# The operands of the final stage: loaded behind the last group of the stage before, in its buffers

## The chip, the core and the metric

The kernel runs on one core of a Trainium2 chip, in one launch. The metric is the device time of that launch in microseconds (us), lower is better. The time before is 6255.53 us, the median of three runs (6249.93 to 6257.06). The profile is of a separate run of 6245.49 us, whose span from first to last instruction is 6243.7 us.

## What is computed

The reference is the forward pass and the gradients of a gated mixture of two attention blocks over one sequence of 2048 tokens with width 576. Block A is attention of 32 heads with 18 channels each, which share one key and one value head. Block B is a recurrence over 64 segments of 32 tokens with 8 memory rows, 32 heads of 128 channels. In short:

```python
g = sigmoid((x * gate_w).sum(-1, keepdims=True))        # x is A_x
a = softmax_attention(x @ wq, x @ wk, x @ wv) @ wo      # block A
b = memory_recurrence(B_x, mem0, Wq, Wk, Wv, Wo)        # block B
out = g * a + (1 - g) * b
grads = vjp(out)(grad_out)   # of A_x, wq, wk, wv, wo, mem0, Wq, Wk, Wv, Wo, gate_w
```

The end of the kernel, which is what matters here, computes the weight gradients of block B, the output and the gate's gradient, and then, for block A:

```
dx     = dq @ wq.T + dkv @ wkv.T + dz * gate_w + dxB    (output 1)
d wq   = x.T @ dq                                       (output 2)
d wk, d wv = x.T @ dkv.T                                (outputs 3 and 4)
d wo   = o.T @ da                                       (output 5)
```

Here dq, dkv, o and da come from the backward pass of block A and lie in DRAM since long before; dz is the gradient of the gate's argument, one number for each token, and dxB is what block B adds.

## The kernel before

The program is a series of stages, each with its own pools of SBUF and PSUM tiles: projections, the forward recurrence woven with attention A, bulk work of B, the backward recurrence woven with the backward pass of A, `b_post`, then the two stages of interest, `b_dw` and `a_final`. A pool is given back at the end of its `with` block, and a later pool may lie on the same memory; its first instructions then wait for whatever still uses that memory.

`b_dw` runs 16 groups, k = 0 to 15: four weight gradients (Wo, Wq, Wk, Wv) by four pairs of column blocks of 512. The contraction is over 20 row tiles, 16 of tokens and 4 of memory rows. Operand one is `w_d`, 128 x 20 x 512 in bf16, with four buffers: two in use and two being loaded, since `load(k + 1)` is issued at the start of group k. Operand two is `w_h`, 128 x 20 x 576 in bf16, with two buffers: one holds db and the memory's gradient for k below 4, the other holds x (`A_x`, its first 16 row tiles) and the memory rows for all groups after. Each group makes nine products (20 matmuls each in the first eight) into the PSUM tile `w_acc` (six buffers of one bank), `evac` copies each out on VectorE (DVE) and ScalarE (ACT) in turn to `w_o16` (four buffers), and GpSimd (POOL) issues the store. After each group `gate(k)` computes row tile k of the output and of dz, from tiles that `gate_load` requested at the group's start: `o_b` and `o_go` through GpSimd, `o_T` through SyncE (SP).

After group 15 the gradient of gate_w is made: `dz_all` is cast to `w_dz`, 32 matmuls multiply it with the x part of `w_h`, two DVE copies make `w_dg` (L1199) and SyncE stores it (L1200).

`a_final` then loads all that it needs (L1623 to L1640): gate_w broadcast over partitions, five token tensors of 128 x 16 x 576 (x, dq, ot, da, dxb, 2304 KB each, on SyncE and GpSimd in turn), wq, wkv and dkv. wkv is made by 20 small loads on GpSimd, with a memset ahead. It transposes wq and wkv on TensorE (PE) (`f_wtr`, one PSUM buffer), brings dkv into token order (`f_pk`), and goes over 16 row tiles for dx: transposes of dq (`f_ptr`, two buffers), products into `f_big` (two buffers of two banks), `f_dx32` on DVE, `f_dx16` on GpSimd, the store on SyncE for even tiles and GpSimd for odd ones. Then, for five row tiles of the weights, it makes the products x.T @ dq, o.T @ da and x.T @ dkv.T.

Within `b_dw` the order of instructions on each engine is that of the program (`manual_schedule`). `a_final` has no such block: there a scheduler orders the instructions when the kernel is built. [...] Matmuls and transposes all pass through two helpers and so carry L66 and L71; copies by `evac` carry L61 (DVE) and L63 (ACT). Their tile names tell them apart.

Of the kernel before, what the change touches and what calls it, by code (L numbers as in the profile page):

```python
# [9 lines left out]
BF16 = mybir.dt.bfloat16  # L10
F32 = mybir.dt.float32
P = 128

D = 576
NKT = 5
# [15 lines left out]
class Kern:  # L31
# [1067 lines left out]
    def b_dw(self, sp, psum):  # L1099
        nc = self.nc  # L1100
        NTT = self.NTT
        n = NTT + self.NM // P
        WS = ("o", "dq", "dk", "dv")

        def load(k):
            which, jp = WS[k // 4], k % 4
            ts = []
            for jc in (2 * jp, 2 * jp + 1):
                cs = slice(jc * 512, (jc + 1) * 512)
                t = sp.tile([P, n, 512], BF16, name="w_d", bufs=4)  # L1110
                nc.sync.dma_start(t[:, 0:NTT, :], self.xtok[which][:, cs].rearrange("(n p) d -> p n d", p=P))
                if k < 4:
                    for mt in range(self.NM // P):
                        nc.sync.dma_start_transpose(
                            t[:, NTT + mt, :].rearrange("p (h e) -> p h e", e=E),
                            self.oh_dram[mt][:, 4 * jc:4 * jc + 4, :].rearrange("e h t -> e (h t)"))
                else:
                    nc.sync.dma_start(t[:, NTT:n, :], self.mtok[which][:, cs].rearrange("(n p) d -> p n d", p=P))
                ts.append((t, cs))
            return ts  # L1120

        def load_h(xs, ms):
            ht = sp.tile([P, n, D], BF16, name="w_h", bufs=2)
            nc.sync.dma_start(ht[:, 0:NTT, :], xs.rearrange("(n p) d -> p n d", p=P))
            nc.sync.dma_start(ht[:, NTT:n, :], ms.rearrange("(n p) d -> p n d", p=P))
            return ht

        def groups(k, ts, ht):
            if k < 4:
                od = self.outs[10].rearrange("h e d -> (h e) d")  # L1130
                for t, cs in ts:
                    for i in range(4):
                        acc = [psum.tile([P, 512], F32, name="w_acc", bufs=6) for _ in range(2)]
                        for it in range(n):
                            for hf in range(2):
                                self.mm(acc[hf][:, 0:288], lhsT=t[:, it, 128 * i:128 * i + 128],
                                        rhs=ht[:, it, 288 * hf:288 * hf + 288], start=(it == 0), stop=(it == n - 1))
                        o16 = sp.tile([P, D], BF16, name="w_o16b", bufs=3)
                        for hf in range(2):
                            self.evac(o16[:, 288 * hf:288 * hf + 288], acc[hf][:, 0:288])  # L1140
                        r0 = cs.start + i * 128
                        nc.gpsimd.dma_start(od[r0:r0 + 128, :], o16[:, :])
                        yield
                return
            od = self.outs[6 + k // 4].rearrange("d h e -> d (h e)")
            for t, cs in ts:
                for kt in range(4):
                    acc = psum.tile([P, 512], F32, name="w_acc", bufs=6)
                    for it in range(n):
                        self.mm(acc[:], lhsT=ht[:, it, kt * P:kt * P + P], rhs=t[:, it, :],  # L1150
                                start=(it == 0), stop=(it == n - 1))
                    o16 = sp.tile([P, 512], BF16, name="w_o16", bufs=4)
                    self.evac(o16[:], acc[:])
                    nc.gpsimd.dma_start(od[kt * P:kt * P + P, cs], o16[:])
                    yield
            acc = psum.tile([P, 512], F32, name="w_acc", bufs=6)
            for it in range(n):
                for i, (t, cs) in enumerate(ts):
                    self.mm(acc[64 * i:64 * i + 64, :], lhsT=ht[:, it, 512:576], rhs=t[:, it, :],
                            start=(it == 0), stop=(it == n - 1), tp=(0, 64 * i))  # L1160
            o16 = sp.tile([P, 512], BF16, name="w_o16", bufs=4)
            self.evac(o16[:], acc[:])
            for i, (t, cs) in enumerate(ts):
                nc.gpsimd.dma_start(od[512:576, cs], o16[64 * i:64 * i + 64, :])
            yield

        with self.tc.manual_schedule():
            ht = load_h(self.db_dram, self.dm_dram)
            nxt = load(0)
            wo = sp.tile([P, NKT, D], BF16, name="w_wo", bufs=1)  # L1170
            nc.vector.memset(wo[64:128, 4, :], 0.0)
            nc.gpsimd.dma_start(wo[:, 0:4, :], self.A_wo[0:512, :].rearrange("(k p) d -> p k d", p=P))
            nc.gpsimd.dma_start(wo[0:64, 4, :], self.A_wo[512:D, :])
            mem = None
            for k in range(16):
                ts = nxt
                if k % 4 == 0 and k < 12:
                    mem = self.mem_tok(k // 4, sp, psum, 2)
                    next(mem)
                if k < 15:  # L1180
                    nxt = load(k + 1)
                if k == 1:
                    hx = load_h(self.A_x, self.mem_dram)
                gl = self.gate_load(k, sp)
                for _ in groups(k, ts, ht):
                    next(mem, None)
                self.gate(k, gl, wo, sp, psum)
                if k == 3:
                    ht = hx
            dz16 = sp.tile([P, NTT], BF16, name="w_dz", bufs=1)  # L1190
            nc.vector.tensor_copy(dz16[:], self.dz_all[:])
            pg = [psum.tile([P, 512], F32, name="w_acc", bufs=6) for _ in range(2)]
            for tt in range(NTT):
                for hf in range(2):
                    self.mm(pg[hf][0:1, 0:288], lhsT=dz16[:, tt:tt + 1], rhs=ht[:, tt, 288 * hf:288 * hf + 288],
                            start=(tt == 0), stop=(tt == NTT - 1))
            dg16 = sp.tile([P, 2, 288], BF16, name="w_dg", bufs=1)
            for hf in range(2):
                nc.vector.tensor_copy(dg16[0:1, hf, :], pg[hf][0:1, 0:288])  # L1199
            nc.sync.dma_start(self.outs[11][None, :], dg16[0:1].rearrange("p a b -> p (a b)"))  # L1200

    def setup_A_dram(self, dram):
        T = self.T
# [412 lines left out]
            for i, (l, r) in enumerate(pairs):  # L1616
                self.mm(out[:, lo:hi], lhsT=l, rhs=r[:, lo:hi], start=(i == 0), stop=(i == n - 1))

    def a_final(self, keep, sp, psum):
        nc = self.nc  # L1620
        T, NTT = self.T, self.NTT
        gwb = keep.tile([P, D], BF16, name="f_gwb")
        nc.sync.dma_start(gwb[:], self.gate_w.partition_broadcast(P))  # L1623
        tok = {}
        for i, (nm, src) in enumerate((("x", self.A_x), ("dq", self.dqtok_dram), ("ot", self.otok_dram),
                                       ("da", self.da_dram), ("dxb", self.dxB_dram))):
            t = keep.tile([P, NTT, D], BF16, name="f_" + nm)
            (nc.sync if i % 2 == 0 else nc.gpsimd).dma_start(t[:], src[:, 0:D].rearrange("(n p) d -> p n d", p=P))
            tok[nm] = t
        wq = keep.tile([P, NKT, D], BF16, name="f_wq")  # L1630
        wkv = keep.tile([P, NKT, P], BF16, name="f_wkv")
        nc.gpsimd.memset(wkv[:], 0.0)
        for kt in range(NKT):
            rows = KT_ROWS[kt]
            r = slice(kt * P, kt * P + rows)
            nc.sync.dma_start(wq[0:rows, kt, :], self.A_wq[r, :])
            for i in range(4):
                nc.gpsimd.dma_start(wkv[0:rows, kt, 32 * i:32 * i + DA], (self.A_wk if i < 2 else self.A_wv)[r, :])
        dkv = keep.tile([P, T], BF16, name="f_dkv")
        nc.sync.dma_start(dkv[:], self.dkv_dram[:, :])  # L1640
        wqT = keep.tile([P, NKT, D], BF16, name="f_wqT")
        wkvT = keep.tile([P, D], BF16, name="f_wkvT")
        for kd in range(NKT):
            drows = KT_ROWS[kd]
            ptr = psum.tile([P, 640], BF16, name="f_wtr", bufs=1)
# [6 lines left out]
            rows = KT_ROWS[kt]  # L1652
            self.tr(ptr[:, kt * P:kt * P + rows], wkv[0:rows, kt, :], rows)
        self.evac(wkvT[:, :], ptr[:, 0:D])
        dkt = keep.tile([P, NTT, 36], BF16, name="f_dkt")
        for t4 in range(NTT // 4):
            pk = psum.tile([P, 4, 36], F32, name="f_pk", bufs=1)
            for j in range(4):
# [34 lines left out]
def build_full(tc, A_x, A_wq, A_wk, A_wv, A_wo, B_mem0, B_Wq, B_Wk, B_Wv, B_Wo, gate_w, grad_out, outs_raw,  # L1693
               dbg=None):
    nc = tc.nc
    T = A_x.shape[1]
# [3 lines left out]
    k = Kern(tc, T, A_x, A_wq, A_wk, A_wv, A_wo, B_mem0, B_Wq, B_Wk, B_Wv, B_Wo, gate_w, grad_out, outs=outs)  # L1700
    PS = lambda name, bufs=1: tc.tile_pool(name=name, bufs=bufs, space=bass.MemoryType.PSUM)
    SB = lambda name, bufs=1: tc.tile_pool(name=name, bufs=bufs)
    with SB("const") as cpool, tc.tile_pool(name="dram", bufs=1, space=bass.MemoryType.DRAM) as dram:
# [38 lines left out]
        with SB("tw") as tw:  # L1742
# [4 lines left out]
                    k.weave(k.b_chain_bwd(rk, rs, rp), k.a_pass2(a3k, a3s, a3p), 1)  # L1747
            with SB("yk") as yk, SB("ys") as ys, PS("yp") as yp:
                k.b_post(yk, ys, yp)
        with SB("ws") as ws, PS("wp") as wp_:  # L1750
            k.b_dw(ws, wp_)
        with SB("a5k") as a5k, SB("a5s") as a5s, PS("a5p") as a5p:
            k.a_final(a5k, a5s, a5p)
    return k


# [74 lines left out]
```

The softmax here doesn't subtract the row's maximum and nothing guards it: scores larger than these inputs give would overflow.

## Time and profile before

| What | Value |
|---|---|
| Time, median of three | 6255.53 us |
| Span of the profiled run | 6243.7 us |
| PE busy over the span | 5691.9 us (91%) |
| DVE, ACT, POOL busy | 60%, 56%, 31% |
| Last group of `b_dw` and its gate on PE, end | about 6104 us |
| Matmuls for the gradient of gate_w | 6106.8 to 6110.9 us |
| Last of the two `w_dg` copies ends | 6111.6 us |
| First transpose of wq (`f_wtr`) | 6153.5 us |
| Last matmul of the kernel ends | 6239.2 us |

Times inside the profile count from the first instruction of the span. In a chain of waits each row gives a start, a duration and the work that held up the end in that time; SPq is the SyncE queue issuing a DMA. In a timeline, the bracket after a row is the idle time before it and what ended that. In the windows, each engine's busy us stand with the number of its instructions in brackets, then the granted TensorE clock (1.00 is full), the share of time in which the 16 DMA engines were busy, and GB/s.

### The profile page before, as it was taken

How to read it: one execution, taken by the hardware profiler on the slowest of the kernel's cores; microseconds unless marked ns; L12 is line 12 of the kernel's file. 1: busy time of each engine (PE TensorE's matmuls, PEld its weight loads, DVE VectorE, ACT ScalarE, POOL GpSimd, SP SyncE). 2: the span in 40 equal slices, each digit the busy share in tenths (PEclk: the TensorE clock that was granted, in tenths of full speed). 3: DMA queues.
4: the chain of work that ended last, by engine and by line, in shares of the span. 5: the costliest groups of instructions: out<-in, count | busy, mean ns of one | idle time of the engine just before them, and what ended most of it. 6: DMA issues, size and time to landing. Idle time of an engine off the chain costs nothing.

```text
span 6243.7 us, 208736 instructions
## 1 busy us (share of the span) xinstructions
PE 5691.9 (91%) x88611; PEld 3321.0 (53%) x88822; DVE 3743.0 (60%) x7061; ACT 3500.1 (56%) x5105; POOL 1952.9 (31%) x3451
## 2 busy tenths in 40 slices
PE   7898999999999985999869999999998999899996
PEld 5443444444444434777735555555554777674443
DVE  4336777777777773666558888888887111121111
ACT  3326787778777873656557777777776222111101
POOL 3002343434343342444423333333333111122213
PEclk9999999999999997999989999999999999999998
DMA  4646666666675536999864444444444999996643
GB/s 153 223 151 120 126 125 127 126 127 125 127 125 107 105 85 181 249 257 258 245 207 107 109 109 108 108 111 109 110 108 103 244 244 250 243 261 196 222 150 114
DMA packets 1368111, 991.97 MB, mean 159 GB/s; under 512 B 931613, under 2 KB 1184806, under 8 KB 1356486
## 3 DMA queue, kind: packets, MB, share of 16 engines
q1 hardware_dynamic: 1285030, 780.53, 52.1%
q0 software_dynamic: 82144, 198.05, 10.0%
q8 instruction: 696, 11.40, 0.8%
q14 instruction: 241, 1.97, 0.1%
HBM read 552.41 MB, written 384.76 MB: 150 GB/s over the span
## 4 chain that ended last, share of the span: by engine, by line
PE 64%; ACT 15%; issue 9%; DMA 6%; SPq 3%; POOL 2%; DVE 1%; ACTq 0%; POOLq 0%; DVEq 0%
ACT b_E L1564 10%; PE w_acc L66 10%; PE a_acc L66 8%; PE c_x L66 6%; PE b_S L66 6%; PE a_S L66 5%; PE c_pj L66 5%; PE p_pb L66 4%; PE r_pj L66 4%; ACT a_E L1422 3%; PE r_x L66 2%; DMA dsx_dram<-x_dS 2%; PE x_tr L71 2%; PE b_acc L66 2%; PE x_po L66 1%
## 5 line engine op out<-in xcount | busy, mean ns | idle before, releaser
L1455 DVE TENSOR_TENSOR a_W<-a_dP,a_E 128x512 bf16<-128x512 f32 x2048 | 1316.2, 685 | 413.2 <-PE a_dP L66 289.7
L1585 DVE TENSOR_TENSOR b_dS<-b_dP,b_E 128x512 bf16<-128x512 f32 x2048 | 1312.9, 683 | 241.8 <-issue 119.6
L1564 ACT ACTIVATE b_E<-b_S 128x1024 bf16<-128x1024 f32 x1024 | 1048.9, 1024 | 446.3 <-PE b_dP L66 322.0
L1422 ACT ACTIVATE a_E<-a_S 128x1024 bf16<-128x1024 f32 x1024 | 1050.6, 1026 | 218.5 <-PE a_dP L66 182.9
L66 PE MATMUL b_S<-b_KV,b_QD 32*128 32x512 bf16 x2048 | 401.1, 382 | 155.2 <-ACT b_E L1564 100.7
L66 PE MATMUL r_pj<-WT,r_dT 128*32 128x288 bf16 x12288 | 493.5, 287 | 1.5 <-issue 1.5
L66 PE MATMUL w_acc<-w_d,w_h 128*128 128x512 bf16 (+1 forms) x2352 | 471.0, 379 | 2.5
L66 PE MATMUL a_acc<-a_E,l_VK 128*32 128x512 bf16 x4096 | 401.6, 380 | 27.9 <-ACT a_acs L1460 27.8
L66 PE MATMUL a_S<-a_QD,l_KV 32*128 32x512 bf16 x2048 | 398.5, 384 | 24.7 <-ACT a_E L1422 15.3
L66 PE MATMUL b_acc<-b_dS,b_SD 128*32 128x512 bf16 x2048 | 419.3, 391 | 0.6 <-DVE b_dS L1585 0.2
L66 PE MATMUL a_acc<-a_W,l_WK 128*32 128x512 bf16 x4096 | 411.8, 390 | 0.2 <-DVE a_W L1455 0.2
L66 PE MATMUL b_acc<-b_E,b_SD 128*32 128x512 bf16 x2048 | 404.0, 391 | 0.0
L66 PE MATMUL b_dP<-b_KV,b_QD 32*128 32x512 bf16 x2048 | 401.2, 386 | 0.0
L66 PE MATMUL a_dP<-a_QD,l_KV 32*128 32x512 bf16 x2048 | 398.1, 385 | 0.0
L66 PEld LDWEIGHTS <-r_dT 128*32 128x32 bf16 x12288 | 333.2, 97 | 80.5 <-issue 2.6
L1055 DVE COPY y_T<-y_pt 128x512 bf16<-128x512 bf16 x256 | 97.1, 420 | 461.5 <-PE y_pt L71 461.4
L66 PEld LDWEIGHTS <-b_QD 32*128 32x128 bf16 x4096 | 164.9, 91 | 345.7 <-issue 284.7
L66 PEld LDWEIGHTS <-w_h 128*128 128x128 bf16 (+1 forms) x2400 | 213.0, 100 | 244.6 <-issue 3.4
L66 PEld LDWEIGHTS <-hm 128*32 128x32 bf16 x7680 | 188.2, 96 | 186.4 <-issue 14.6
L1041 ACT CAST y_tdk<-y_pk 128x512 bf16<-128x512 f32 x128 | 75.1, 587 | 377.0 <-PE y_pk L66 212.5
L66 PEld LDWEIGHTS <-l_KV 32*128 32x128 bf16 x4096 | 118.9, 91 | 297.4 <-issue 275.3
L66 PE MATMUL y_pdx<-WT,y_T 128*128 128x288 bf16 x2048 | 272.8, 287 | 0.0
(416 smaller groups left out, 11401.9 us busy)
## 6 DMA issues: line engine op xcount, KB each, us to landing
b_QD<-qd_dram SPq DMA_DIRECT2D x256, 128.0 KB
b_SD<-sd_dram SPq DMA_DIRECT2D x256, 128.0 KB
dOx_dram<-p_tok SPq DMA_DIRECT2D x16, 1024.0 KB
c_vx<-vx_dram SPq DMA_DIRECT2D x256, 64.0 KB
krow_dram<-c_k POOLq DMA_DIRECT2D x64, 256.0 KB, 3.0
qrow_dram<-c_q POOLq DMA_DIRECT2D x64, 256.0 KB, 3.4
vrow_dram<-c_v POOLq DMA_DIRECT2D x64, 256.0 KB, 3.0
x_q<-qx_dram SPq DMA_DIRECT2D x32, 512.0 KB
```

The lines of the kernel that those rows point to most:

```text
L66: return self.nc.tensor.matmul(out, lhsT, rhs, start=start, stop=stop, tile_position=tp, skip_group_check=True)
L71: return self.nc.tensor.transpose(out, in_, self.identB[b:b + nrows, b:b + nrows], tile_position=tp)
L1041: nc.scalar.copy(d[w][:, r, :], pk[:])
L1055: nc.vector.tensor_copy(T_[t][w][:], pt[:])
L1422: nc.scalar.activation(E_[n][:], S.pop(n)[:], ACT.Exp, scale=SCALEA)
L1455: nc.vector.tensor_tensor(out=W_[n][:, i, :], in0=dP[i][:], in1=E_[n][:, i, :], op=ALU.mult)
L1564: nc.scalar.activation(E_[n][:], S.pop(n)[:], ACT.Exp, scale=SCALEA)
L1585: nc.vector.tensor_tensor(out=D_[n][:, i, :], in0=dP[i][:], in1=E_[n][:, i, :], op=ALU.mult)
```

## The change

The change lets the final stage take its operands from the buffers of the weight-gradient stage, which stay alive for it, so that loads can be issued before that stage is over.

- x is not loaded a second time: `tok["x"]` is the `w_h` tile that the stage still holds.
- At the start of group 15, after `gate_load`, `final_load` takes the other `w_h` buffer, in which db lay, and packs wq, gate_w, dkv and wkv into it. It also requests dq and dxb into the next two `w_d` buffers.
- After the gradient of gate_w, `final_tok` requests ot and da, which take the last two `w_d` buffers.
- All of these but the small loads of wkv are issued by SyncE; before, dq and da were issued by GpSimd.
- The SBUF pool of `b_dw` stays open around `a_final`; only its PSUM pool is closed. The pool `a5k` is gone; the transposed weights and `f_dkt` lie in `a5s`.

```diff
                 gl = self.gate_load(k, sp)
+                if k == 15:
+                    self.final_load(sp)
                 for _ in groups(k, ts, ht):
...
             nc.sync.dma_start(self.outs[11][None, :], dg16[0:1].rearrange("p a b -> p (a b)"))
+            self.ftok["x"] = ht
+            self.final_tok(sp, ("ot", "da"))
...
-    def a_final(self, keep, sp, psum):
-        gwb = keep.tile([P, D], BF16, name="f_gwb")
-        nc.sync.dma_start(gwb[:], self.gate_w.partition_broadcast(P))
-        tok = {}
-        for i, (nm, src) in enumerate((("x", self.A_x), ("dq", self.dqtok_dram), ("ot", self.otok_dram),
-                                       ("da", self.da_dram), ("dxb", self.dxB_dram))):
-            t = keep.tile([P, NTT, D], BF16, name="f_" + nm)
-            (nc.sync if i % 2 == 0 else nc.gpsimd).dma_start(t[:], src[:, 0:D].rearrange("(n p) d -> p n d", p=P))
-            tok[nm] = t
+    def final_tok(self, ws, names):
+        src = {"dq": self.dqtok_dram, "ot": self.otok_dram, "da": self.da_dram, "dxb": self.dxB_dram}
+        for nm in names:
+            t = ws.tile([P, self.NTT + self.NM // P, 512], BF16, name="w_d", bufs=4)
+            v = t[:].rearrange("p a b -> p (a b)")[:, 0:self.NTT * D].rearrange("p (n d) -> p n d", d=D)
+            self.nc.sync.dma_start(v, src[nm][:, 0:D].rearrange("(n p) d -> p n d", p=P))
+            self.ftok[nm] = v
+    def final_load(self, ws):
+        f = ws.tile([P, self.NTT + self.NM // P, D], BF16, name="w_h", bufs=2)
+        flat = lambda r, n: f[:, r:, :].rearrange("p a b -> p (a b)")[:, 0:n]
+        wq, gwb = f[:, 0:NKT, :], f[:, NKT, :]
+        dkv = flat(6, self.T)
+        wkv = flat(10, NKT * P).rearrange("p (k c) -> p k c", c=P)
+        nc.gpsimd.memset(wkv, 0.0)
         for kt in range(NKT):
...
             nc.sync.dma_start(wq[0:rows, kt, :], self.A_wq[r, :])
             for i in range(4):
                 nc.gpsimd.dma_start(wkv[0:rows, kt, 32 * i:32 * i + DA], (self.A_wk if i < 2 else self.A_wv)[r, :])
+        nc.sync.dma_start(dkv, self.dkv_dram[:, :])
+        nc.sync.dma_start(gwb, self.gate_w.partition_broadcast(P))
+        self.final_tok(ws, ("dq", "dxb"))
...
-        with SB("ws") as ws, PS("wp") as wp_:
-            k.b_dw(ws, wp_)
-        with SB("a5k") as a5k, SB("a5s") as a5s, PS("a5p") as a5p:
-            k.a_final(a5k, a5s, a5p)
+        with SB("ws") as ws:
+            with PS("wp") as wp_:
+                k.b_dw(ws, wp_)
+            with SB("a5s") as a5s, PS("a5p") as a5p:
+                k.a_final(a5s, a5p)
```

More of the change, by code (lines that the diff above doesn't have):

```diff
@@ L1617, in row_mm @@
                 self.mm(out[:, lo:hi], lhsT=l, rhs=r[:, lo:hi], start=(i == 0), stop=(i == n - 1))
-    def a_final(self, keep, sp, psum):
-        nc = self.nc
-        T, NTT = self.T, self.NTT
-        gwb = keep.tile([P, D], BF16, name="f_gwb")
-        nc.sync.dma_start(gwb[:], self.gate_w.partition_broadcast(P))
-        tok = {}
-        for i, (nm, src) in enumerate((("x", self.A_x), ("dq", self.dqtok_dram), ("ot", self.otok_dram),
-                                       ("da", self.da_dram), ("dxb", self.dxB_dram))):
-            t = keep.tile([P, NTT, D], BF16, name="f_" + nm)
-            (nc.sync if i % 2 == 0 else nc.gpsimd).dma_start(t[:], src[:, 0:D].rearrange("(n p) d -> p n d", p=P))
-            tok[nm] = t
-        wq = keep.tile([P, NKT, D], BF16, name="f_wq")
-        wkv = keep.tile([P, NKT, P], BF16, name="f_wkv")
-        nc.gpsimd.memset(wkv[:], 0.0)
+    ftok = {}
+    def final_tok(self, ws, names):
[6 more added lines that the diff above has]
+    def final_load(self, ws):
+        nc = self.nc
+        f = ws.tile([P, self.NTT + self.NM // P, D], BF16, name="w_h", bufs=2)
[4 more added lines that the diff above has]
+        nc.gpsimd.memset(wkv, 0.0)
         for kt in range(NKT):
@@ L1638, in a_final @@
                 nc.gpsimd.dma_start(wkv[0:rows, kt, 32 * i:32 * i + DA], (self.A_wk if i < 2 else self.A_wv)[r, :])
[L1639 to L1642, printed above, removed]
+        nc.sync.dma_start(dkv, self.dkv_dram[:, :])
+        nc.sync.dma_start(gwb, self.gate_w.partition_broadcast(P))
+        self.final_tok(ws, ("dq", "dxb"))
+        self.fin = (gwb, wq, wkv, dkv)
+    def a_final(self, sp, psum):
+        nc = self.nc
+        T, NTT = self.T, self.NTT
+        gwb, wq, wkv, dkv = self.fin
+        tok = self.ftok
+        wqT = sp.tile([P, NKT, D], BF16, name="f_wqT", bufs=1)
+        wkvT = sp.tile([P, D], BF16, name="f_wkvT", bufs=1)
         for kd in range(NKT):
@@ L1654, in a_final @@
         self.evac(wkvT[:, :], ptr[:, 0:D])
-        dkt = keep.tile([P, NTT, 36], BF16, name="f_dkt")
+        dkt = sp.tile([P, NTT, 36], BF16, name="f_dkt", bufs=1)
         for t4 in range(NTT // 4):
```

## The prediction

> **What bounds the kernel now.** I began with the page: its 40 slices show TensorE (PE) at 8 or 9 tenths nearly everywhere and at 6 in the last, so the end of the span has something of its own. The change touches only the last 180 us, so I read the chain of waits from 6095 us, where each row is start, duration and what held the end back:
>
> ```profile
> 6106.77 3.97 PE w_acc L66 x31
> 6111.14 0.45 DVE w_dg L1199
> 6111.60 1.12 DMA out_dram<-w_dg
> 6112.81 0.37 SPq L1623
> 6113.23 0.42 SPq L1628
> 6113.69 5.26 SPq L1628
> 6118.99 19.13 SPq L1628
> 6138.16 7.98 SPq L1636
> ...
> 6147.16 7.61 DMA f_wq<-in_A_wq_dram
> 6154.82 0.47 PE f_wtr L71 x2
> ```
>
> From 6111.60 the chain leaves the compute engines: the store of the gate-weight gradient, gate_w (L1623), the three of the five big loads that SyncE issues behind each other (L1628; GpSimd issues dq and da), wq (L1636), and only then the first transposes of wq. The windows of that stretch say what the engines did meanwhile (length, then busy us and count of PE, weight loads, DVE, ACT, POOL, then granted clock, DMA share, GB/s):
>
> ```profile
> 6104.00:6111.00 7.00, 4.08 (x32) 2.60 (x32) 2.85 (x9) 0.00 (x0) 1.30 (x3) 1.00 0.15 41
> 6111.00:6153.00 42.00, 3.24 (x20) 1.97 (x20) 1.01 (x4) 1.17 (x2) 13.62 (x23) 0.55 0.99 304
> 6153.00:6166.00 13.00, 10.78 (x104) 6.17 (x107) 3.52 (x8) 3.83 (x8) 1.65 (x3) 0.76 0.12 37
> 6166.00:6200.00 34.00, 33.26 (x271) 16.45 (x275) 13.71 (x31) 6.70 (x14) 26.26 (x30) 1.00 0.19 63
> 6200.00:6240.00 40.00, 39.02 (x316) 20.71 (x317) 4.47 (x6) 3.19 (x5) 2.08 (x3) 1.00 0.12 40
> ```
>
> For 42 us the DMA engines are full (0.99, 304 GB/s) and PE works 3.24 us. Afterwards PE is full again (33.26 of 34, 39.02 of 40). So the final stage is a bare load, then PE. The PE timeline gives the edges and what ended each idle time:
>
> ```profile
> 6129.35 1.62 PE L71 MATMUL f_ptr<-identB,f_dq 128*128 128x128 bf16 x10 [18.51 <-issue]
> 6131.23 1.62 PE L71 MATMUL f_ptr<-identB,f_dq 128*128 128x128 bf16 x10 [0.26 <-DVE f_T L61]
> 6153.47 0.29 PE L71 MATMUL f_wtr<-identB,f_wq 128*128 128x128 bf16 x1 [20.62 <-DMA f_wq<-in_A_wq_dram]
> ```
>
> The two waits, 18.51 and 20.62 us, are the prize; between them dq had landed and four row tiles of it were transposed.
>
> [...] in 6027 to 6032 us the loads of the last group of the weight-gradient stage ran at DMA share 1.07 and 386 GB/s, and PE was busy 5.00 of 5.00 us. [...] that stretch came from SyncE nearly alone, while the 354 to 359 GB/s of 6120 to 6135 us came from SyncE and GpSimd together; moving dq and da to SyncE costs no bandwidth. [...] 0.55 in the gap, 0.76 in the 13 us after it, 1.00 beyond; the 2.79 us wait for w_dz at 6104 us left it at 1.00.
>
> **The change part by part.**
> 1. *x is not loaded again* (2304 KB), since w_h still holds it for the gate-weight gradient. No cost.
> 2. *wq, wkv, dkv, gate_w, dq and dxb are issued when group 15 starts.* dq and dxb take the w_d buffers of group 14, which PE left at 6063.7, when the DMA transpose of o_T for group 15 issued. Bytes: 2 x 2304 KB, 648 KB of wq, 512 KB, 144 KB: 6.0 MB. At 350 GB/s that is 17 us; PE's group ends at 6104, so there are 40 us. In 6070 to 6104 the DMA share was about 0.1. All land near 6083. Cost on the path: none; the matmuls of the group hide them.
> 3. *The pool no longer begins on the released memory of the earlier one.* Before, the first load waited for the whole pool, the store of w_dg included (1.12 us). Now PE's first transpose waits for operands long landed, and for the last w_dg copy at 6111.60, because the PSUM pool is handed over as before. Start about 6111.75 instead of 6153.47: **-41.7 us**.
> 4. *The 20 transposes of dq done in the gap* move into the busy part. Later tens take 1.06 us against 1.62 here: **+2.0 us** (two times 1.0).
> 5. *The cold start goes.* The first five wq transposes took from 6153.47 to 6155.28, partly waiting for wq's last rows; later fives take 0.53. That is 1.3 saved, and the next round (0.75 against 0.53) and the first f_big (0.63 against about 0.4) give 0.4 more: **-1.7 us**. The rounds of f_wtr still go through one PSUM buffer and one evacuation each (0.64 on ACT, 0.46 on DVE), but in the built order the dq transposes stand between them, which fills waits such as the 0.73 and 0.33 us at 6156: **-0.6 us**.
> 6. *ot and da* are issued after the w_dg store, at about 6112, into the buffers of group 15. 4.7 MB at 350 GB/s: landed near 6126. Their first reader is the first product of the two, which stood 50 us after the first f_wtr (6203.59 less 6153.47), so at about 6161. Hidden by 35 us.
> 7. *The stores of dx on SyncE stand behind ot and da.* The first is due near 6123, and lands after 6126. Two dx16 buffers, two dx32 buffers and two PSUM tiles give six row tiles, at 2.6 us each 15 us, before PE would wait. Cost: none.
> 8. *20 small wkv loads on GpSimd* stand in front of group 15's w_o stores. Issues cost 0.54 us each, 11 us, and at most eight are in flight: the GpSimd timeline shows that engine stopping after eight for the oldest to land.
>
> ```profile
> 6118.75 1.06 POOL L1638 DMA_DIRECT2D f_wkv<-in_A_wk_dram x2
> 6129.34 0.54 POOL L1638 DMA_DIRECT2D f_wkv<-in_A_wv_dram x1 [9.52 <-DMA f_dq<-dqtok_dram]
> 6137.81 0.54 POOL L1638 DMA_DIRECT2D f_wkv<-in_A_wv_dram x1 [7.94 <-DMA f_da<-da_dram]
> ```
>
> The queue behind: w_o stores, so w_o16 buffers (four), so evacuations, so PSUM (six w_acc banks), so PE. Lower bound: GpSimd is free at 6067 + 0.65 (memset) + 11 = 6079, nothing lost. Upper bound: the 31 us which memset and loads took before, free at 6098; groups 5 to 7 then sit unevacuated in three of six banks, and nine stores of 0.54 us catch up by 6104: up to 3 us at the gate's evacuations. I take 0, and keep 3.
> 9. *The order at the end:* the last 16 f_pk (64x36) now follow the last f_big and their result leaves by two GpSimd stores, each 0.55 us and landing in 2.1, instead of one f_o store: **+0.3 us**.
>
> Sum: -41.7 + 2.0 - 1.7 - 0.6 + 0.3 = **-41.7 us**, and 6255.5 - 41.7 = **6214 us**.
>
> **The rivals.**
> *A new wait takes part of the place (6222).* If ot and da drained at half of 350 GB/s, they would land at 6112 + 27 = 6139 and the first dx store 2 us later; PE, six tiles ahead, would stop at 6123 + 15 = 6138. That is 3 us, with the 3 us of point 8[...]: 8 lost. For it: everything is on one queue. Against: 386 GB/s from that queue.
> *The buffers come free late (6245).* If dq and dxb had to wait for group 15's own w_d, 9.4 MB would start at 6104 and take 27 us, then the stage would start near 6143: 10 us gained. Against: four buffers in rotation, and the next two are group 14's.
> *GpSimd holds up group 15 (6286).* If the 20 small loads passed one at a time, at the 5.2 us which is their median landing before, GpSimd would be free at 6067 + 104 = 6171. Four w_o16 buffers and six banks fill, the gate waits, and the 6111.6 of the w_dg copy becomes about 6171 + 2 (landing) + 3 (five evacuations) + 8 (6104 to 6111.6) = 6184: +72, -41.7, slower by 30. Against: eight in flight, as the lines above show.
>
> **How the numbers follow.** The forecast: 86 in 100. New wait: 9. Late buffers: 2. GpSimd: 3. Faster by over 0.2% (12.5 us, under 6243) takes in the first two, 0.95; 6245 is the no-change case, 0.02; slower 0.03. The forecast's own width is a gain of 38 to 45 us (points 4, 5 and 8 at their ends), 6210.5 to 6217.5, and the three timed runs before spread from 6249.9 to 6257.1, some 4 us to each side. With the first rival inside: 6206 to 6225.
>
> **What would show it.** In the profile after: first f_wtr within 1 us of the last w_dg copy; granted clock 1.00 across the border; dq, dxb, wq, dkv issued within a few us of 6064 and landed before 6090; DMA share about 1 in 6065 to 6083 with PE still full; ot and da landed some 30 us ahead of their first product; span near 6202. It is wrong if PE idles over 2 us between last w_dg and the first f_big, if the f_dx instructions wait for a store, or if the w_o evacuations of group 15 wait for DMAs and the w_dg copy slips from 6111.6.

## The result, and the profile after

The changed kernel takes 6214.59 us (median of six runs, 6212.52 to 6220.47) beside 6254.82 us before (six runs, 6248.08 to 6262.60) in the same comparison: a ratio of 0.9938, 95% interval 0.9925 to 0.9951, or 40 us (31 to 47). In a later comparison it was 0.9942 (0.9929 to 0.9954).

The change touches only the end of the program, while the time at which that end begins differs from run to run: the `o_T` transpose of group 15 ended at 6064.93 us in the profile before and at 6074.23 us after, with nothing changed ahead of it (over all twelve profiles it lies between 6059.95 and 6086.59). So I compare stretches from that point on. Each ends at an event that the PE or the DVE timeline shows.

| Stretch, us | before | after |
|---|---|---|
| `o_T` of group 15 to the gate's last matmul | 39.04 | 39.05 |
| to the end of the last `w_dg` copy | 7.60 | 9.27 |
| to the first `f_wtr` transpose | 41.90 | 0.15 |
| to the first product with `wkvT` | 10.20 | 8.24 |
| to the first x.T @ dq product | 36.00 | 38.01 |
| to the end of the last `f_big` | 39.56 | 39.56 |
| to the end of the span | 4.47 | 7.29 |
| sum | 178.77 | 141.57 |

The sum falls by 37.2 us. The gap is gone whole (41.75), one more stretch is 2.0 us shorter, and three gave back 1.7, 2.0 and 2.8 us. The windows of the profile after show the border (columns as before: length, busy us and count of PE, weight loads, DVE, ACT, POOL, clock, DMA share, GB/s):

```profile
6074.30:6080.00 5.70, 5.70 (x28) 2.61 (x27) 1.87 (x6) 0.00 (x0) 3.87 (x7) 1.00 0.94 241
6085.00:6090.00 5.00, 5.00 (x25) 2.25 (x23) 0.69 (x1) 0.00 (x0) 3.01 (x6) 1.00 1.10 325
6095.00:6100.00 5.00, 5.00 (x24) 2.24 (x23) 0.14 (x1) 0.00 (x0) 1.62 (x3) 1.00 0.88 296
...
6115.00:6122.60 7.60, 5.75 (x32) 3.23 (x32) 1.76 (x7) 0.00 (x0) 0.57 (x1) 0.78 0.06 19
6122.60:6127.00 4.40, 3.90 (x45) 2.60 (x46) 0.92 (x4) 2.62 (x6) 0.00 (x0) 1.00 0.65 185
6127.00:6132.00 5.00, 4.91 (x44) 2.70 (x44) 1.38 (x4) 1.02 (x2) 0.00 (x0) 1.00 1.09 362
```

The full DMA system that stood alone from 6111 to 6153 us before now stands in the first three rows, with PE busy throughout. Its second part, ot and da, stands beside the new start (last two rows). The clock of 0.78 in the fourth row belongs to the `w_dz` matmuls. In the PE timeline the bracket again gives the idle time and what ended it:

```profile
6116.08 5.75 PE L66 MATMUL w_acc<-w_h,w_dz 128*1 128x288 bf16 x32 [2.80 <-DVE w_dz L1193]
6122.70 0.52 PE L71 MATMUL f_wtr<-identB,w_h 128*128 128x128 bf16 x5 [0.87 <-DVE w_dg L1201]
...
6143.28 1.34 PE L66 MATMUL f_big<-f_wqT,f_T 128*128 128x512 bf16 x5 [0.54 <-DVE f_dx L1685]
```

The first `f_wtr` waits for the last `w_dg` copy and for nothing else, as forecast; before, this idle time was ended by a load. The third line is new: PE waits for the sum of dx. The table of waits of the last 146 us (who waited for whom, us in total, times, longest) shows the chain behind it:

```profile
DVE w_o L61 <- DMA out_dram<-w_o: 13.2, 1, 13.2
DVE f_dx L1685 <- POOL f_dx L1688: 11.9, 7, 4.1
POOL f_dx L1688 <- DMA out_dram<-f_dx: 9.9, 6, 4.3
...
PE f_big L66 <- DVE f_dx L1685: 1.7, 4, 0.5
```

From the bottom: PE waited four times for DVE, DVE for GpSimd, and GpSimd for the store of an earlier tile. In the profile before, PE didn't wait for the sum of dx at all, and the two waits behind it were short:

```profile
DVE f_dx L1669 <- POOL f_dx L1672: 1.7, 1, 1.7
POOL f_dx L1672 <- DMA out_dram<-f_dx: 1.2, 1, 1.2
```

In the table after, the first line belongs to group 15, where evacuations waited for `w_o16` buffers behind the small loads; PE did not notice (39.05 us).

### The profile page after: what moved, and what is told of

The parts are those of the page before. It is cut to its first block, busy times and chain, and to the rows that moved or that the text cites. A ratio compares the mean times of both kernels' runs of the same rounds, so it can differ in the third digit from the quotient of the medians.

```text
span 6215.8 us, 208700 instructions
## 1 busy us (share of the span) xinstructions
PE 5692.8 (92%) x88611; PEld 3324.0 (53%) x88822; DVE 3742.9 (60%) x7061; ACT 3497.0 (56%) x5105; POOL 1944.6 (31%) x3449
## 4 chain that ended last, share of the span: by engine, by line
PE 64%; ACT 15%; issue 10%; DMA 6%; POOL 2%; SPq 2%; DVE 1%; POOLq 0%; ACTq 0%; DVEq 0%
ACT b_E L1568 10%; PE w_acc L66 10%; PE a_acc L66 8%; PE c_x L66 6%; PE b_S L66 6%; PE a_S L66 5%; PE c_pj L66 5%; PE p_pb L66 4%; PE r_pj L66 4%; DMA dsx_dram<-x_dS 3%; ACT a_E L1426 3%; PE r_x L66 2%; PE b_acc L66 2%; PE x_tr L71 2%; PE x_po L66 1%
## 5 line engine op out<-in xcount | busy, mean ns | idle before, releaser
L66 PEld LDWEIGHTS <-w_h 128*128 128x128 bf16 (+1 forms) x2688 | 230.0, 100 | 258.3 <-issue 6.6
```

What stands on the lines that cost most here:

```text
L66: return self.nc.tensor.matmul(out, lhsT, rhs, start=start, stop=stop, tile_position=tp, skip_group_check=True)
```

## Experiments

The theory: the gap was transfer time in front of an idle PE, and the kernel gains because these transfers now pass under the matmuls of group 15. The rivals: the gap was long because wq stood last in its queue (order); or the second load of x and the wait for the released pool made it (bytes and hand-over).

**Late issue.** The requests of `final_load` move behind the `w_dg` store; all else as changed.

```diff
-                if k == 15:
-                    self.final_load(sp)
...
             self.ftok["x"] = ht
+            self.final_load(sp)
             self.final_tok(sp, ("ot", "da"))
```

> The changed kernel with one part undone: wq, wkv, dkv, gate_w, dq and dxb are requested after the store of the gate-weight gradient instead of at the start of group 15; x still stays, buffers and order of requests are those of the changed kernel. Theory 'early issue' (the 42 us gap was transfer time, and only issuing it under group 15 removes it all): PE waits for 1.3 MB of small operands and dq (2.4 MB), 3.7 MB at 350 GB/s or 10.5 us plus 2 us latency, with some 6 us of transposes and f_pk fitting in; later the dx stores stand behind dxb, ot and da until about 6111.6 + 33 = 6145 and cost about 4 us more. Some 12 to 14 us of the gain are lost: about 6228. Theory 'no second load of x and no wait for the pool': these alone give 6.7 + 1.1 us, so about 6247. Theory 'order' (wq merely stood last in its queue): nearly all of the gain stays, 6214 to 6218.

Measured: 6238.18 us beside 6265.12 before, ratio 0.9954 (0.9937 to 0.9972). By stretches, 109.6 us from the `w_dg` copy to the end, beside 132.1 before and 93.25 after: 16.3 of the 38.9 us are lost. That is nearest to "early issue", 2 to 4 us beyond it. (The 2 us of latency in it are about what the quiet stores of dx and `f_k` took to land in the profile before, 2.2 and 2.1 us in the median.) The PE timeline of this run shows where PE stood:

```profile
6137.95 0.23 PE L71 MATMUL f_wtr<-identB,w_h 128*128 128x128 bf16 x1 [3.36 <-DMA w_h<-in_A_wq_dram]
...
6155.52 0.64 PE L66 MATMUL f_pk<-f_dkt,w_h 128*128 128x36 bf16 x16 [4.73 <-ACT f_k L63]
6157.51 0.46 PE L66 MATMUL f_pk<-f_dkt,w_h 128*64 128x36 bf16 x6 [1.36 <-DVE f_k L61]
```

The waits for wq came to 5.7 us in all, of which the first row is the longest. Those for copies of `f_k` came to 6.3: in this build the x.T @ dkv.T products stand ahead of the dq transposes, and their results leave through two `f_k16` buffers by stores of 4.5 KB, which took 6.5 us to land in the full DMA system (the median of this run). PE stood behind them in its order. How much of the excess is due to this order wasn't measured.

In time, this kernel's interval overlaps that of the changed kernel (0.9925 to 0.9951). So what early issue is worth rests on the stretches, one profile of each kernel here; two profiles of the changed kernel, the one above and one at the end of this part, agree within 0.1 us.

**Order alone.** The kernel before, with its late requests in another order and all large ones on SyncE: wq, dkv, gate_w, dq, x, dxb, ot, da.

```diff
-        gwb = keep.tile([P, D], BF16, name="f_gwb")
-        nc.sync.dma_start(gwb[:], self.gate_w.partition_broadcast(P))
-        tok = {}
-        for i, (nm, src) in enumerate((("x", self.A_x), ("dq", self.dqtok_dram), ("ot", self.otok_dram),
-                                       ("da", self.da_dram), ("dxb", self.dxB_dram))):
-            t = keep.tile([P, NTT, D], BF16, name="f_" + nm)
-            (nc.sync if i % 2 == 0 else nc.gpsimd).dma_start(t[:], src[:, 0:D].rearrange("(n p) d -> p n d", p=P))
-            tok[nm] = t
...
         nc.sync.dma_start(dkv[:], self.dkv_dram[:, :])
+        gwb = keep.tile([P, D], BF16, name="f_gwb")
+        nc.sync.dma_start(gwb[:], self.gate_w.partition_broadcast(P))
+        tok = {}
+        for nm, src in (("dq", self.dqtok_dram), ("x", self.A_x), ("dxb", self.dxB_dram), ("ot", self.otok_dram),
+                        ("da", self.da_dram)):
+            t = keep.tile([P, NTT, D], BF16, name="f_" + nm)
+            nc.sync.dma_start(t[:], src[:, 0:D].rearrange("(n p) d -> p n d", p=P))
+            tok[nm] = t
```

> The kernel before with only the order of its late requests changed, all on SyncE: wq, dkv, gate_w, dq, then x, dxb, ot, da (before: gate_w, x, ot, dxb, wq, dkv on SyncE and dq, da on GpSimd). Theory 'order': most of the gap goes, since PE needs only wq and dq to begin: first dq transposes about 12.5 us after the w_dg store lands, x 7 us after that, dxb another 7, da at about 6151; with dx stores held behind da I work out about 6225, a gain of 25 to 30 us of the 40. Theory 'early issue': the bytes still come after group 15, so at least the 12.5 us to dq, and the stores behind 12 MB; 6225 to 6238. Theory 'no second load of x': order is worth nothing, 6253. The difference between this kernel and the late-issue one (about 6228) is what the second load of x and the wait for the pool cost, 5 to 10 us if they matter.

Measured: 6246.50 us beside 6265.12, ratio 0.9970 (0.9956 to 0.9983); 118.45 us from the `w_dg` copy to the end. Order alone is worth 13.7 of the 38.9 us, half of what I gave it, because the bytes that remain meet the same small stores and, through them, the dx loop: its stretch to the first x.T @ dq product took 50.3 us instead of 36.0, with 8.9 us of idle PE, 6.2 of them for copies of `f_k`.

The two together split the gain along this path: order 132.1 - 118.45 = 13.7 us; no second load of x and no wait for the released pool 118.45 - 109.6 = 8.9 us (7.8 expected from 6.7 of transfer and 1.1 of store); early issue 109.6 - 93.25 = 16.3 us. No rival makes the whole gain; early issue is the largest part and the one that the others can't replace. Two things blur the split. The kernel with late issue and the one with the other order also differ in the order that the scheduler gave them (only in the first do all x.T @ dkv.T products stand ahead of dx), so the 8.9 us are not those two causes alone. And the changed kernel pays 3.3 us more at its end than either (see below on the end of the span); up to the end of the last `f_big` the three parts are 13.1, 9.0 and 19.6 us.

The next five kernels ran once each (6222.80, 6225.06, 6216.56, 6223.80 and 6211.93 us, in the order in which they stand here). Single times spread more than the effects in question (those of the changed kernel from 6201 to 6221), so I read only the stretches of their profiles.

**Four dx16 buffers.** The first of two runs on the wait for dx.

```diff
-            dx16 = sp.tile([P, D], BF16, name="f_dx16", bufs=2)
+            dx16 = sp.tile([P, D], BF16, name="f_dx16", bufs=4)
```

> The changed kernel with four f_dx16 buffers instead of two. In its profile PE waits four times for DVE f_dx, 1.7 us in all, DVE for GpSimd f_dx 11.9 us, and GpSimd for the store of f_dx 9.9 us. If two buffers make a loop of sum, store and landing that can't catch up after a slow store: these waits all but vanish and the stretch from the first product with wkvT to the first x.T dq product shrinks from 38.0 to about 36.5 us. If GpSimd itself is the limit (1.27 us a tile and its issues), nothing changes.

Measured: the stretch is 35.94 us instead of 38.01, and no wait of PE for dx is left.

**No load of ot and da.** The second.

```diff
-            self.final_tok(sp, ("ot", "da"))
+            self.ftok["ot"] = self.ftok["da"] = self.ftok["dq"]
```

> The changed kernel without the loads of ot and da: the product for output 5 takes dq for both operands, so that output isn't the reference's. If the dx loop waits because its stores stand behind 4.7 MB in a full DMA system: the waits for f_dx vanish as with four buffers, and the stretch from the first product with wkvT to the first x.T dq product is about 36 us instead of 38.0. If two f_dx16 buffers are too few even for quiet stores (2.2 us to land): it stays at 37 to 38 us.

Measured: 35.93 us, with two buffers. So both conditions are needed: with 4.7 MB in flight the first store by GpSimd took 4.74 us in the changed kernel, where GpSimd waited 9.9 us in all for stores of dx beside 2.0 in this run, and with two buffers the loop can't run ahead of it. The GpSimd timeline of the changed kernel shows the first such turn, a store issued at 6136.23 for which the sum of a later tile waits until 6141.11; in the quiet dx loop before, a store landed in 2.2 us:

```profile
6136.23 0.54 POOL L1689 DMA_DIRECT2D out_dram<-f_dx  x1
6141.11 1.27 POOL L1688 TENSOR_TENSOR f_dx<-f_dx,w_d 128x576 bf16<-128x576 f32 x1 [4.34 <-DMA out_dram<-f_dx]
...
6144.74 2.52 POOL L1688 TENSOR_TENSOR f_dx<-f_dx,w_d 128x576 bf16<-128x576 f32 x2
...
6149.22 2.50 POOL L1688 TENSOR_TENSOR f_dx<-f_dx,w_d 128x576 bf16<-128x576 f32 x2 [1.48 <-DMA out_dram<-f_dx]
...
6153.72 2.50 POOL L1688 TENSOR_TENSOR f_dx<-f_dx,w_d 128x576 bf16<-128x576 f32 x2 [1.49 <-DMA out_dram<-f_dx]
```

The last two rows are 8 and 13 us later, when ot and da had long landed, and still wait: two sums (2.50) and about 2.0 us until a store has landed make a turn of 4.5 us for two tiles. PE, where nothing held it up, took 5.0 to 5.1 us for two (the four-buffer run). So the loop is a little faster than PE, but wins back only some 0.6 us in each turn of the 4.34 that it waited at the first; PE met it four times, the last at 6155.88.

**The end of the span.** The stores of `f_k` on SyncE.

```diff
-            nc.gpsimd.dma_start(self.outs[3][cs, :], k16[0:drows, 0:DA])
-            nc.gpsimd.dma_start(self.outs[4][cs, :], k16[0:drows, DA:36])
+            nc.sync.dma_start(self.outs[3][cs, :], k16[0:drows, 0:DA])
+            nc.sync.dma_start(self.outs[4][cs, :], k16[0:drows, DA:36])
```

> The changed kernel with the stores of the wk and wv gradients (f_k) issued by SyncE instead of GpSimd. In its profile 7.3 us pass from the end of the last f_big to the end of the span, before 4.5 us. If the two GpSimd issues and the slower end after them make the difference: about 5 us, a gain of 2.3. If the 16 f_pk after the last f_big make it: no more than 0.5 us of change.

Measured: 5.03 us from the last `f_big` to the end, instead of 7.29. The SyncE waits of the last 9.5 us, first of the changed kernel, then of this one (the last line number of each is the end of the program):

```profile
SPq L1843 <- PEq L1843: 3.3, 2, 2.8
SPq L1843 <- DMA out_dram<-f_k: 1.9, 1, 1.9
```

```profile
SPq L1843 <- DMA out_dram<-f_o: 0.7, 1, 0.7
SPq L1843 <- PEq L1843: 0.7, 2, 0.5
```

The difference lies in the end of the program itself: 3.3 us after a last store by GpSimd, 0.7 after a last store by SyncE. It was 0.6 or 0.7 in every run whose last store was by SyncE. After a last store by GpSimd it was 3.3 us in four profiles and 5.1 in the run of the next experiment. Why the end takes longer then wasn't tried. The dx stretch shrank too, by 1.1 us (36.92); the issues of `f_k` no longer stand between the sums on GpSimd, but whether that is the reason wasn't tried apart.

**Twice the small loads.** Each of the 20 loads of wkv issued twice.

```diff
-            for i in range(4):
+            for i in (0, 1, 2, 3, 0, 1, 2, 3):
```

> The changed kernel with each of the 20 small loads of wkv issued twice in group 15 (40 instead of 20). With 20, GpSimd was free 18 us after the first of them, the evacuations waited 13.2 (DVE) and 9.3 us (ACT) for w_o16 buffers, and the group with its gate took 39.05 us against 39.04 before, so buffers and PSUM banks took it all up. If this slack has an end: 40 take about 35 us, so stores of the group start 36 us into it, PE has filled four buffers and six banks by its tenth product, and the gate waits; group and gate about 43 us, the w_dg copy some 4 to 7 us later. If something else absorbs it (the loads pass faster, or the wait isn't on this path): 39.05 us again.

Measured: group and gate 42.36 us instead of 39.05. The PE and wait views of this run:

```profile
6114.02 2.32 PE L66 MATMUL w_acc<-w_wo,o_T 128*128 128x288 bf16 x9 [2.10 <-DVE w_o L61]
```

```profile
DVE w_o L61 <- DMA out_dram<-w_o: 28.7, 3, 26.9
ACT w_o L63 <- DMA out_dram<-w_o: 23.8, 2, 23.2
```

The slack has an end, and where it was expected: with 13 and 9 us of waiting evacuations four buffers and six banks hide all, with 28.7 and 23.8 PE stops at the gate. The stores of `w_o` stand behind all the loads in GpSimd's order: the first one of the group went out at 6110.95, against 6094.27 in the changed kernel. The `w_dg` copy came 4.6 us later.

**Transposes in the idle time.** wq and wkv are transposed after the gate of group 15, into `w_acc` tiles, ahead of `w_dz`.

```diff
+            self.final_wT(sp, psum)
             dz16 = sp.tile([P, NTT], BF16, name="w_dz", bufs=1)
...
+    def final_wT(self, sp, psum):
...
+        for kd in range(NKT + 1):
+            drows = KT_ROWS[kd] if kd < NKT else P
+            ptr = psum.tile([P, 1024], BF16, name="w_acc", bufs=6)
+            for kt in range(NKT):
+                rows = KT_ROWS[kt]
+                src = wq[0:rows, kt, kd * P:kd * P + drows] if kd < NKT else wkv[0:rows, kt, :]
+                self.tr(ptr[0:drows, kt * P:kt * P + rows], src, rows)
+            self.evac(wqT[0:drows, kd, :] if kd < NKT else wkvT[:, :], ptr[0:drows, 0:D], use="s")
...
```

> The changed kernel with the transposes of wq and wkv moved in the program between the gate of group 15 and the gate-weight gradient, into w_acc tiles, evacuated by ACT alone. PE idles 2.8 us there for w_dz (DVE chain of the gate). 30 transposes at 0.53 us for five are 3.1 us, so they fill the idle time; after the w_dg copy only dq transposes, f_pk and f_big remain. Expected if PE order is what costs: the stretch from the w_dg copy to the first product with wkvT shrinks from 8.4 to about 5 us, and the end of the gate's matmuls to the w_dg copy grows by at most 0.4. If the chain of evacuations is what costs, not PE: no more than 1 us.

Measured: the gap of 2.8 us is filled, the gate's end to the `w_dg` copy is 7.60 us, and from there to the first `wkvT` product 3.0 us instead of 8.4. But the stretch after it took 44.1 us instead of 38.0. Part of both is work that changed sides: ten transposes of dq and some products, about 2.1 us, now stand behind the first `wkvT` product, and so do the last 16 `f_pk` (the end of the span shrank to 4.0 us, with a last store by SyncE). The rest is the dx loop. Windows of this run:

```profile
6139.00:6142.00 3.00, 2.24 (x44) 1.65 (x44) 0.32 (x2) 0.77 (x2) 1.83 (x3) 1.00 0.01 2
6142.00:6145.00 3.00, 2.10 (x5) 0.51 (x4) 1.63 (x2) 0.00 (x0) 3.00 (x5) 0.58 0.29 98
6145.00:6150.00 5.00, 5.00 (x25) 1.98 (x25) 1.28 (x4) 1.02 (x2) 4.57 (x7) 0.57 0.22 63
```

PE stopped for GpSimd (1.10 us in one piece), and the clock fell to 0.57. GpSimd had waited 4.96 us for a store of dx, and then 4.64 us at a store of `f_k` whose copy wasn't made yet, with two sums of dx behind it in its order. From the `w_dg` copy to the end of the last `f_big` it is 86.7 us, beside 86.0 in the changed kernel: by itself the edit turns its gain in front of the dx loop into waits in it.

**All three edits.** Transposes in the idle time, four dx16 buffers, `f_k` stores on SyncE.

> The changed kernel with three edits at once: wq and wkv transposed ahead of the gate-weight gradient, four f_dx16 buffers, f_k stores on SyncE. Each is worth what it was worth alone if they lie on different stretches: 2.1 us (dx loop), 2.3 us (end of the span), 3.4 us (transposes in the idle time); from the end of the o_T transpose of group 15 to the end of the span 141.6 - 7.8 = about 134 us. As a time 6207 beside 6214.6 for the changed kernel; a ratio of about 0.9925 to the kernel before. If the dx loop and the end hang together (the stores on SyncE now stand in the dx stores' queue), 1 to 2 us less.

Measured: 6214.43 us beside 6258.58, ratio 0.9930 (0.9917 to 0.9944), which doesn't part it from the changed kernel. By stretches 132.6 us instead of 141.6, of which 1.7 are the clock of the `w_dz` matmuls (see the next part). So both ran again, side by side:

> The changed kernel once more, beside the one with the three edits on the same chip, since their ratios to the kernel before (0.9938 and 0.9930) came from different comparisons and overlap. Expected: 0.993 to 0.994 again. In the profile, the 32 matmuls with w_dz take 4.1 or 5.75 us: if the slow ones are chance and no part of the change, either may be seen; all other stretches from the o_T transpose of group 15 on repeat within 0.2 us.

> The kernel with the three edits once more, on the same chip. By the stretches of its profile (132.6 us against 141.6 from the o_T transpose of group 15 to the end, of which 1.7 is the clock of the w_dz matmuls) it should be 7 to 9 us faster than the changed kernel: a ratio to the kernel before lower by 0.0011 to 0.0014. If the gain is given back elsewhere in the run: equal ratios.

Measured: 6208.98 us (ratio 0.9942, 0.9929 to 0.9954) for the changed kernel and 6196.12 us (0.9921, 0.9907 to 0.9934) for the three edits, beside 6246.91 before. The intervals overlap a little, but the medians are 13 us apart, the slowest of the five runs with three edits (6200.47) is faster than the fastest of the changed kernel (6201.36), and the stretches repeat: 141.64 and 132.35 us, each within 0.3 of its first run. In this kernel PE stands at 35.93 of 36 us in the dx stretch:

```profile
6119.70:6125.00 5.30, 5.02 (x48) 2.69 (x48) 1.89 (x6) 1.63 (x4) 0.56 (x1) 1.00 0.72 219
6125.00:6161.00 36.00, 35.93 (x307) 17.71 (x304) 14.53 (x29) 7.81 (x16) 21.99 (x22) 1.00 0.48 159
```

The transposes that gave nothing by themselves are worth about 3.2 us here: from the `w_dg` copy to the end of the last `f_big`, 83.9 us with the four buffers alone and 80.7 with all three edits. Whether the buffers or the `f_k` stores that left GpSimd made room for them wasn't tried apart.

## Why the prediction was right, point by point

The forecast of 6214 us met 6214.6, and the 41.7 us met 40 by the medians and 37.2 by this pair of profiles. The agreement of the total is closer than that of its terms, four of which missed by 1.7 to 2.5 us, three one way and one the other; that it came within 1 us is luck, and the 37.2 us lie just below the 38 to 45 that the prediction gave as its own width.

- *The hand-over (3), -41.7:* measured -41.75, with the first `f_wtr` 0.15 us after the `w_dg` copy. This is the step that carries the forecast.
- *Early loads hidden by group 15 (2), 0:* 0.01 us. I had them landed 19 us into the group; the DMA system stayed full for about 26 (share 0.88 in 6095 to 6100), since it moved 241 to 325 GB/s there and not 350. The 13 us left before the gate's end made this harmless.
- *dq transposes, cold start, rounds (4, 5), -0.3 in sum:* measured -2.0, of which 0.6 are 16 `f_pk` that the built order moved to the end of the kernel. The likely reason for the rest, not tried apart: the transposes moved in were hidden in the waits for evacuations better than I had it.
- *ot and da hidden (6), 0:* right for their readers, since the DMA share fell from 1.09 to 0.42 after 6137 and the first product of the two began at 6172.88.
- *dx stores behind them (7), 0:* wrong. It cost 2.0 us, and the run without ot and da and the one with four buffers each bring 2.1 back. The failing step was to count six tiles as 15 us of slack. PE did stop at the seventh tile, but it got there at 6142.74, 11.0 us after the first sum on DVE: the transposes of four tiles had been done ahead, so that its first six tiles ended within 10.0 us. And the store that the loop waited for landed at 6140.97, not soon after ot and da; the loop then won back only 0.6 us in a turn. This is my first rival, at a quarter of its size; 2 of its 8 us were for a slower clock after the wait, an estimate that no measured number stood behind.
- *Small loads on GpSimd (8), 0 with 3 as bound:* right. GpSimd was done with them 17.4 us after the memset began, between the 12 and 31 us of the bounds, and twice the loads showed that the limit is near.
- *The end (9), +0.3:* measured +2.8. The 0.5 us of `f_pk` only moved there; the mis-sized term is the end of the program, which took 3.3 us after a GpSimd store instead of 0.7, and which nothing in the profile before showed.
- *Not in the sum, the clock:* the 32 `w_dz` matmuls took 5.75 us instead of 4.08, after the same 2.8 us of idle time. I had read 2.79 us as harmless, from the one profile before, where the clock stayed at 1.00, and from an estimate of my own; the measurement decides against that. It isn't the change's doing either: of the seven profiles with that idle time (2.79 to 2.80 us), the kernel before and the four-buffer one had 4.08, and five others 5.75, among them the order experiment, where everything up to there is the kernel before. The clock records of two of the traces, before and after, can be laid side by side. In both, the shortest stretch at one clock lasts 3.41 us and every other one that ends inside the span a whole multiple of that, so both can be cut into steps of 3.41 us. In the profile after a step begins within 0.1 us of the gate's last matmul and holds the whole idle time; in the profile before it begins 0.74 us after that matmul and holds 2.05 us of it. Windows cut along these steps, two of the profile after and one of the profile before:

```profile
6113.30:6116.70 3.40, 0.62 (x6) 0.43 (x7) 2.62 (x8) 0.00 (x0) 1.34 (x3) 1.00 0.31 82
6116.72:6120.10 3.38, 3.38 (x17) 1.81 (x15) 0.00 (x0) 0.00 (x0) 0.00 (x0) 0.50 0.00 0
...
6104.72:6108.10 3.38, 1.33 (x11) 0.92 (x12) 1.90 (x6) 0.00 (x0) 0.58 (x2) 1.00 0.32 85
```

  After the step with 0.62 us of PE work came one at a clock of 0.50; after the one with 1.33 us the clock stayed at 1.00. That is one case of each, no run was made to test it, and busy time alone doesn't order the cases: in the run with the transposes alone, 2.24 us of PE work in the 3 us from 6139 were followed by 3 us at 0.58.
- *The signs that it named:* the first `f_wtr`, the early requests and the landing of ot and da (36 us ahead of their first product) came as described; a clock of 1.00 across the border did not. The span was 6215.8 us and not 6202, 9.3 of it because group 15 began later in that run. Two signs of being wrong came as well: sums of dx waited for a store, which is point 7, and evacuations of group 15 waited for DMAs, which PE did not notice.
- *The second rival's sum* doesn't come out as written: 27 us from 6104 end at 6131, and the step to 6143 isn't given. The runs don't need it, since dq and dxb found their buffers free.

## What to carry to other kernels

When a stage begins with loads while the matmul engine idles, keep the pool of the stage before alive and put the loads into buffers that have run out of use; what must come first goes first, and order alone was 13.7 of the 38.9 us here. Then look at what shares the DMA system with the last loads: here stores that landed in 2.1 to 2.2 us in the quiet took 4.7 (dx) and 6.5 us (`f_k`, with late issue) beside them, and a loop with two buffers became the new wait, although with quick stores it was a little faster than PE (4.5 us for two tiles, beside 5.0 to 5.1). Compare stretches between fixed events when a change is smaller than the spread of whole runs.

## What the runs showed that I had not expected

- The end of the program took 3.3 us of waiting after a last GpSimd store (5.1 in one of five profiles) and 0.6 or 0.7 after a last SyncE store (seven profiles).
- After an idle time of 2.8 us the `w_dz` matmuls took 5.75 us in five profiles and 4.08 in two, with PE's instructions up to there the same; the profile after shows a clock of 0.50 for 3.41 us there, the profile before 1.00 throughout. With the gap filled (three profiles) they took 4.08 us each time.
- Stores of 4.5 KB took 6.5 us to land (median) with 2304 KB loads in flight, and issues on SyncE behind such loads held its queue for 5.26, 19.13 and 7.98 us in the kernel before.
